# State-space scan with a feed-forward layer on one core: new durations in the table from which the order of issue is planned

## Chip, cores and metric

One core of one Trainium2 chip. The metric is the device time of one execution in microseconds (us), smaller is better. The kernel before takes 324.34 us (median of 3 runs, 323.94 to 324.47).

## What is computed

A linear state-space scan in chunks, and a feed-forward layer on its output. From the reference:

```python
batch, n_heads, seq, head_dim, d_state = (4, 8, 768, 32, 16)   # x, a, B, C in float32
for c in range(nc):                    # chunks along the sequence
    cum = np.cumsum(log(a)[c], axis=-1)
    L = np.exp(cum[:, :, :, None] - cum[:, :, None, :]) * causal
    y = (np.einsum('bhin,bhjn->bhij', Cc, Bc) * L) @ xc  +  (Cc @ state) * np.exp(cum)
    state = exp(sum(la)) * state + sum_j exp(cum[-1] - cum[j]) * B[j] x[j]
# x: (3072, 256) from y;  w_in (256, 2048), w_out (2048, 256): float64 in, float32 arithmetic here
h = x @ w_in
g = h - np.tanh(h)
out = g @ w_out
```

## The kernel before

**The scan.** The sequence is cut into 28 chunks (4 batches, 7 chunks of at most 112 tokens). The state of the chunk before enters a chunk as 16 extra rows of its `x` tile. TensorE makes, for chunks 0 to 3, the exponents of the decays (`cp`, lines 448 and 451) and the products of B and C (`att`, line 461). For chunks 4 to 9 one `att` tile gets both (lines 507 and 512). ScalarE takes the exponential into a tile `lt` (467, 516, 550), VectorE multiplies `lt` by `att` in place (471, 520, 684), GpSimd zeroes what is not causal (532, called the cut here), and TensorE multiplies `lt` by `x` into `y` (637, from chunk 10 on two chunks at once in 704) and the states into the next chunk's rows (644, or 572 into a tile `z`). `att` and `y` use the array in pieces of 32 rows or columns. ScalarE copies the new states into the rows of a later `x` tile (578 out of `z`, 650 out of `y`).

**The layer.** The output of the scan is split into a high and a low float32r half, `xh` by ScalarE (605, 617) and `xl` by VectorE (608, 619). 3,072 tokens are cut into 4 tiles of 256 and 4 of 512. For each tile and each of 16 slices of the hidden width, TensorE makes `ph` (763 with three products of halves, 756 in plain float32 for the first tile and the first weights), ScalarE takes tanh (794) and VectorE subtracts it (798) into `g`; `g` is split (802, 808), and TensorE adds `g` times w_out into `o` (844; 834 in plain float32 for the first weights). ScalarE copies partial sums out of `o` (872 into `pt`, 885).

**The weights.** They arrive as float64 words in `raw`, and are made into float32 by a chain: ScalarE 325, VectorE 330, 335, 338, 345. Then ScalarE makes the high half `wh` (349) and VectorE the low half `wl` (352). The first two of eight weight blocks are loaded and converted in two halves each, w_in first; the second half of these stays in float32 as `wf`.

**The order.** Nothing is issued as it is written. Each piece of work is first recorded with its engine, a duration in us, what it reads and what it writes:

```python
op("PE", 0.65, fn_p, r=[d["n_bc"], "lt_c", "rt_c"], w=[n_a])
op("ACT", 0.92, fn_e, r=[n_a], w=n_l)
op("DVE", 1.08, fn_m, r=[n_a], w=n_l)
op("POOL", 1.4, lambda: cut(ck), w=n_l)
```

`Order.schedule` (line 136 on) plays these records against each other: an engine takes, of the work that is ready, the piece with the smallest priority; a transfer occupies one common lane for bytes / `RATE` after a fixed start, and its data may be used `DMA_LATENCY` later. `Order.search` repeats this forward and backward 16 times with priorities jittered by a random generator (`SEED`), and keeps the pass that ends first; `issue` then emits every instruction in the order of its start. On the chip each engine, and SyncE's queue of transfers, works through its own instructions strictly in this order. A planned start is not enforced: only the order is, and semaphores hold an instruction until its inputs, and the buffer that it writes, are free. Buffers that matter below: two banks `ph`, one bank each of `po0`, `po1` (for `z`, `y` and `o` in turn) and one set of banks `att`, so that the next `att` waits until VectorE has read the last one.

Of the kernel before, what the change touches and what calls it, by code (L numbers as in the profile page):

```python
# [63 lines left out]
class Order:  # L64
# [3 lines left out]
    DMA_LATENCY, SEM, SEM_PE, RATE, FLIGHT = 0.8, 0.15, 0.28, 0.32e6, 8  # L68
    ROUNDS, JITTER, SEED, EARLY, LOOK = 16, 0.3, 266, 8.0, 0.5
# [19 lines left out]
    def __call__(self, eng, cost, fn, r=(), w=(), dma=0, after=(), urge=0.0):  # L89
# [33 lines left out]
        if dma:  # L123
            self.urge.append(urge)

            self.ops.append(("DMA", max(0.25, dma / self.RATE), None, {i: 1.4, **{j: 0.0 for j in chain}}))
# [9 lines left out]
    def schedule(self, prio, back=False, hold=None):  # L136
# [18 lines left out]
        while done < n:  # L155
# [67 lines left out]
def tile_ssm_moe(ctx: ExitStack, tc: tile.TileContext, a, x, bn, bc, wts, out):  # L223
# [90 lines left out]
    def conv(u, halves=False):  # L314
# [63 lines left out]
    def prep(G):  # L378
# [18 lines left out]
        op("POOL", 0.3, fn_c, r=["idn"], w=[d["n_bc"]])  # L397
        if near:
            op("POOL", 0.8, fn_b, r=["wdec", "bi", d["n_b"]], w=[d["n_bw"]])
# [35 lines left out]
    def first_tile():  # L435
# [38 lines left out]
        for ck in range(FIRST):  # L474
# [5 lines left out]
            for i in range(2):  # L480
                n_f, n_k = slot("ph", NPH), slot("g", 3)
                op("POOL", 0.7, lambda ck=ck, i=i: fn_k(ck, i), r=["la"], w=[n_k], urge=urge)
                op("PE", 1.14, lambda ck=ck, i=i: fn_f(ck, i), r=[n_k, "upto", "never"], w=[n_f])
                op("ACT", 0.52, lambda ck=ck, i=i: fn_x(ck, i), r=[n_f, "tab"], w=[k["n_l"][i]], urge=urge)
# [9 lines left out]
    def chunk_a(ck):  # L494
# [27 lines left out]
        op("PE", 0.65, fn_p, r=[d["n_bc"], "lt_c", "rt_c"], w=[n_a])  # L522
# [12 lines left out]
    def chunk_l(ck):  # L535
# [87 lines left out]
    def chunk_y(ck):  # L623
# [29 lines left out]
        cost = 0.48 if apart else 0.68  # L653
# [35 lines left out]
    def pair_y(ck):  # L689
# [51 lines left out]
    def mm1(t, f):  # L741
# [32 lines left out]
        op("PE", 12 * rate(w) * blocks(t), fn, r=[*n, f"wh{f // 2}.0", f"wl{f // 2}.0"], w=[n_h])  # L774
# [43 lines left out]
    def mm2(t, f, seg):  # L818
# [30 lines left out]
        if native(t, f):  # L849
            op("PE", 6.8 * 0.25 * blocks(t) / 2, fn, r=[*n_in, f"wf{f // 2}"], w=n_po[t, seg])  # L850
# [164 lines left out]
    for w in range(2):  # L1015
        op("DVE", 0.85, lambda w=w: signs(w), r=["par"], w=["rt_c"])
# [47 lines left out]
    op("PE", 0.95, sums_rows, r=["la", "upto"], w=[n_pr])  # L1064
    op("PE", 0.55, lambda: sums_cols(upto, "pq"), r=["la", "upto"], w=[n_pr])
# [3 lines left out]
    op("DVE", 1.4, lambda: [split(i) for i in range(1, 6) if i != 4], r=["rows"], w=["parts"])  # L1069
# [6 lines left out]
    op("ACT", 0.22, lambda: nc.scalar.activation(wdec.rearrange("p h c -> p (h c)"), misc["pq2"][:, 0:NHC], AF.Exp),  # L1076
# [123 lines left out]
```

## Time and profile before

| | |
|---|---|
| median of 3 runs | 324.34 us |
| the profiled execution, its own time | 324.25 us |
| its span | 322.6 us |
| TensorE, matmuls | 313.7 us, 97% of the span |
| VectorE | 215.3 us, 67% |
| ScalarE | 210.3 us, 65% |
| GpSimd | 60.6 us, 19% |
| transfers | 35.27 MB |

The span counts from the first to the last instruction of the core; 1.65 us of the time lie around it. Engines are named PE (TensorE), DVE (VectorE), ACT (ScalarE), POOL (GpSimd) and SP (SyncE, which issues transfers). L763 is line 763 of the kernel. A matmul on 4-byte data shows as two instructions in the trace where the order has one. Busy times of TensorE overlap from one matmul to the next; the chain of waits counts end to end instead.

### The profile page before, as it was taken

How to read it: one execution, taken by the hardware profiler on the slowest of the kernel's cores; microseconds unless marked ns; L12 is line 12 of the kernel's file. 1: busy time of each engine (PE TensorE's matmuls, PEld its weight loads, DVE VectorE, ACT ScalarE, POOL GpSimd, SP SyncE). 2: the span in 40 equal slices, each digit the busy share in tenths (PEclk: the TensorE clock that was granted, in tenths of full speed). 3: DMA queues.
4: the chain of work that ended last, by engine and by line, in shares of the span. 5: the costliest groups of instructions: out<-in, count | busy, mean ns of one | idle time of the engine just before them, and what ended most of it. 6: DMA issues, size and time to landing. Idle time of an engine off the chain costs nothing.

```text
span 322.6 us, 5757 instructions
## 1 busy us (share of the span) xinstructions
PE 313.7 (97%) x2160; PEld 255.3 (79%) x2160; DVE 215.3 (67%) x314; ACT 210.3 (65%) x471; POOL 60.6 (19%) x94
## 2 busy tenths in 40 slices
PE   8997999999999999999999999999999999999995
PEld 7765888788888878787878887888878788888883
DVE  6978997898888867457563864664765645645552
ACT  6568888477687888575945854966868544534451
POOL 8604424003122514402300400111102000000000
PEclk9999999999999999999999999999999999999999
DMA  6679557539433149280606005005420000100001
GB/s 205 195 238 325 173 162 307 183 94 346 89 65 66 30 98 272 48 241 5 205 0 207 16 0 209 1 2 226 168 61 0 2 0 0 68 1 0 2 0 65
DMA packets 15451, 35.27 MB, mean 109 GB/s; under 512 B 2464, under 2 KB 4416, under 8 KB 15424
## 3 DMA queue, kind: packets, MB, share of 16 engines
q1 hardware_dynamic: 13696, 31.76, 29.4%
q0 software_dynamic: 1728, 3.15, 5.7%
q8 instruction: 17, 0.28, 0.4%
q14 instruction: 10, 0.08, 0.1%
HBM read 28.32 MB, written 3.43 MB: 98 GB/s over the span
## 4 chain that ended last, share of the span: by engine, by line
PE 91%; DVE 5%; ACT 2%; issue 1%
PE ph L763 39%; PE o L844 38%; PE o L834 3%; PE y L704 3%; PE att L678 3%; PE y L637 1%; PE warm L1003 1%; DVE lt L471 1%; ACT lt L550 1%; DVE lt L520 1%; DVE wv L345 1%; PE att L461 1%; PE cp L451 1%; ACT lt L516 1%; DVE wm L338 1%
## 5 line engine op out<-in xcount | busy, mean ns | idle before, releaser
L798 DVE TENSOR_TENSOR g<-ph,g 128x512 f32<-128x512 f32 x96 | 65.7, 688 | 52.1 <-ACT g L794 52.0
L794 ACT ACTIVATE g<-ph 128x512 f32<-128x512 f32 x96 | 57.3, 598 | 48.7 <-PE ph L763 47.8
L808 DVE TENSOR_TENSOR gl<-g,gh 128x512 fp32r<-128x512 f32 x88 | 62.7, 715 | 31.0 <-ACT gh L802 29.5
L763 PE MATMUL ph<-xh,wh 128*128 128x512 f32 (+1 forms) x200 | 76.0, 382 | 0.0
L763 PE MATMUL ph<-xh,wl 128*128 128x512 f32 (+1 forms) x200 | 74.8, 377 | 0.0
L802 ACT CAST gh<-g 128x512 fp32r<-128x512 f32 x88 | 54.4, 620 | 28.3 <-DVE g L798 26.4
L844 PE MATMUL o<-gh,wh 128*128 128x512 f32 x176 | 69.2, 393 | 0.0
L844 PE MATMUL o<-gl,wh 128*128 128x512 f32 x176 | 68.5, 389 | 0.0
L844 PE MATMUL o<-gh,wl 128*128 128x512 f32 x176 | 68.5, 389 | 0.0
L763 PE MATMUL ph<-xl,wh 128*128 128x512 f32 (+1 forms) x200 | 59.0, 376 | 0.0
L532 POOL TENSOR_SCALAR_AFFINE_SELECT lt<-lt 128x896 f32<-128x896 f32 (+1 forms) x24 | 23.3, 969 | 128.4 <-ACT lt L550 118.3
L763 PEld LDWEIGHTS ph<-xh,wh 128*128 128x128 f32 x200 | 37.6, 188 | 7.6 <-issue 0.6
L763 PEld LDWEIGHTS ph<-xh,wl 128*128 128x128 f32 x200 | 37.6, 188 | 6.8
L763 PEld LDWEIGHTS ph<-xl,wh 128*128 128x128 f32 x200 | 36.7, 188 | 7.0
L550 ACT ACTIVATE lt<-lt,ncum 128x112 f32<-128x112 f32 (+1 forms) x144 | 41.7, 375 | 0.0
L844 PEld LDWEIGHTS o<-gh,wh 128*128 128x128 f32 x176 | 33.0, 188 | 7.8 <-issue 0.8
L844 PEld LDWEIGHTS o<-gl,wh 128*128 128x128 f32 x176 | 33.0, 188 | 6.9
L844 PEld LDWEIGHTS o<-gh,wl 128*128 128x128 f32 x176 | 33.1, 188 | 6.7
L684 DVE TENSOR_TENSOR lt<-att,lt 128x896 f32<-128x896 f32 (+1 forms) x18 | 18.9, 1052 | 0.0
L888 POOL DMA_DIRECT2D pt<-part x12 | 11.1, 1023 | 41.1 <-ACT part L885 38.1
L834 PE MATMUL o<-g,wf 128*128 128x256 f32 x64 | 15.4, 384 | 1.4 <-ACT x L578 0.9
L605 ACT CAST xh<-y 128x224 fp32r<-128x224 f32 (+4 forms) x18 | 7.3, 413 | 13.1 <-DVE s L711 10.6
(97 smaller groups left out, 275.0 us busy)
## 6 DMA issues: line engine op xcount, KB each, us to landing
lt<-cumr SPq DMA_DIRECT2D x18, 512.0 KB
raw<-w_d SPq DMA_DIRECT2D x16, 512.0 KB
bc<-bc_d SPq DMA_DIRECT2D x14, 352.0 KB
x<-x_d SPq DMA_DIRECT2D x14, 256.0 KB
pt<-part POOLq DMA_DIRECT2D x12, 256.0 KB, 4.5
out_d<-ob SPq DMA_DIRECT2D x8, 256.0 KB
braw<-bn_d SPq DMA_DIRECT2D x14, 112.0 KB
out_d<-pt SPq DMA_DIRECT2D x4, 256.0 KB
```

Of the source, the lines that this page charges most:

```text
L532: nc.gpsimd.affine_select(out=k["l"][:, :, 0:q], in_=k["l"][:, :, 0:q], pattern=[[0, H], [1, q]], compare_op=ALU.is_ge, fill=0.0, base=N, ...
L550: nc.scalar.activation(k["l"][:, h, 0:q], k["l"][:, h, 0:q], AF.Exp, bias=ncum[:, h, ck : ck + 1])
L678: nc.tensor.matmul(out=a_[:, i], lhsT=bb[r], rhs=cc[r, :, 0 : qlen(ck)], start=True, stop=True)
L684: nc.vector.tensor_tensor(out=l, in0=chs[j]["a"], in1=l, op=ALU.mult)
L763: nc.tensor.matmul(out=ph[:, i * w : i * w + w], lhsT=w_[:, u, 0, k, j * P : (j + 1) * P], rhs=(xh, xl)[p][:, k, ts], start=p == 0 and k = ...
L794: nc.scalar.activation(g[:, 0:used], gs[t, f][0][:, 0:used], AF.Tanh)
L798: nc.vector.tensor_tensor(out=g, in0=ph, in1=g, op=ALU.subtract)
L802: nc.scalar.copy(gh[:, 0:used], gs[t, f][1][:, 0:used])
L808: nc.vector.tensor_tensor(out=gl[:, 0:used], in0=g[:, 0:used], in1=gh[:, 0:used].bitcast(F32), op=ALU.subtract)
L834: nc.tensor.matmul(out=po[t, seg][e], lhsT=wf[:, u, 256 * j + e * P : 256 * j + (e + 1) * P], rhs=gs[t, f][1][:, i * w : i * w + w], start ...
L844: nc.tensor.matmul(out=po[t, seg][e], lhsT=w_[:, u, 1, j, e * P : (e + 1) * P], rhs=g[:, i * w : i * w + w], start=f == seg[0] and k == 0 ...
L888: op("POOL", 1.0, lambda e=e: nc.gpsimd.dma_start(out=pts[m][:, e], in_=obs[t, e], accum_op=ALU.add), r=[name, n_pt[2 * m], n_pt[2 * m + 1 ...
```

## The change

No instruction is added or removed. The recorded durations are replaced, the fixed start of a transfer becomes a name of its own (1.4 us before, now 0.65 us, with 0.45 us instead of 0.8 us behind the data and a lower rate), and the seed of the search is another. With other numbers the search ends in another order. The core of the diff (some 25 more durations change like the last ones shown):

```diff
-    DMA_LATENCY, SEM, SEM_PE, RATE, FLIGHT = 0.8, 0.15, 0.28, 0.32e6, 8
-    ROUNDS, JITTER, SEED, EARLY, LOOK = 16, 0.3, 266, 8.0, 0.5
+    DMA_START, DMA_LATENCY, SEM, SEM_PE, RATE, FLIGHT = 0.65, 0.45, 0.15, 0.28, 0.29e6, 8
+    ROUNDS, JITTER, SEED, EARLY, LOOK = 16, 0.3, 2, 8.0, 0.5
...
-                start[i + 1] = max(free["DMA"], end + 1.4)
+                start[i + 1] = max(free["DMA"], end + self.DMA_START)
...
-        op("POOL", 1.4, lambda: cut(ck), w=n_l)
+        op("POOL", 0.97, lambda: cut(ck), w=n_l)
...
-            op("PE", 6.88 * 0.25 * blocks(t) / 2, fn, r=[*n, convs[f // 2]], w=[n_h])
+            op("PE", 7.7 * 0.25 * blocks(t) / 2, fn, r=[*n, convs[f // 2]], w=[n_h])
```

What the new numbers do is seen in the order of each engine. In the rows below a line has the line number, the operation, what is written <- what is read, and the shape; a number at the end of a name is that of the buffer, and counts up in each program by itself.

**First place: SyncE's queue at the very start**, right after the load of `a`: the loads of B and C (`bc`), of `x`, of the first half of the first weights (`raw`, 512 KB) and of B again (`braw`). Before:

```order
L265 DMA bc_136<-bc_d 128x704
L265 DMA bc_138<-bc_d 128x704
L296 DMA raw_147<-w_d 128x1024
L277 DMA x_156<-x_d 128x512
L277 DMA x_158<-x_d 128x512
L265 DMA bc_160<-bc_d 128x704
L286 DMA braw_106<-bn_d 112x256
```

Now:

```order
L265 DMA bc_136<-bc_d 128x704
L277 DMA x_151<-x_d 128x512
L265 DMA bc_154<-bc_d 128x704
L296 DMA raw_159<-w_d 128x1024
L286 DMA braw_106<-bn_d 112x256
L277 DMA x_165<-x_d 128x512
L265 DMA bc_171<-bc_d 128x704
```

One `x` load (256 KB) now stands ahead of the first weights, and `braw` has come forward.

**Second place: VectorE and ScalarE while chunks 4 to 6 and the second weight block are worked on** (some 23 to 32 us of the trace before). `lt_433` before is `lt_430` now, chunk 5; `lt_513` is `lt_516`, chunk 6; `g_0_408` is `g_0_482`, the first slice of the layer; `wm` and `wv` belong to the conversion of the second weight block. VectorE before:

```order
L345 SCALAR_TENSOR_TENSOR wv_389<-wv_389,wm_410 128x512
L520 TENSOR_TENSOR lt_433<-att_416,lt_433 128x8x112
L798 TENSOR_TENSOR g_0_408<-ph_0_377,g_0_408 128x512
L330 TENSOR_SCALAR wm_410<-raw_328 128x512
L335 TENSOR_SCALAR wv_389<-wv_389 128x512
L338 SCALAR_TENSOR_TENSOR wm_410<-wv_389,wm_410 128x512
L619 TENSOR_TENSOR xl<-xf,xh 128x2x336
L520 TENSOR_TENSOR lt_513<-att_491,lt_513 128x8x112
L608 TENSOR_TENSOR xl<-y_453,xh 128x2x112
L345 SCALAR_TENSOR_TENSOR wf<-wv_389,wm_410 128x512
```

VectorE now:

```order
L345 SCALAR_TENSOR_TENSOR wv_388<-wv_388,wm_407 128x512
L520 TENSOR_TENSOR lt_430<-att_413,lt_430 128x8x112
L330 TENSOR_SCALAR wm_407<-raw_338 128x512
L335 TENSOR_SCALAR wv_388<-wv_388 128x512
L338 SCALAR_TENSOR_TENSOR wm_407<-wv_388,wm_407 128x512
L798 TENSOR_TENSOR g_0_482<-ph_0_375,g_0_482 128x512
L619 TENSOR_TENSOR xl<-xf,xh 128x2x336
L345 SCALAR_TENSOR_TENSOR wf<-wv_388,wm_407 128x512
L608 TENSOR_TENSOR xl<-y_450,xh 128x2x112
L520 TENSOR_TENSOR lt_516<-att_490,lt_516 128x8x112
```

ScalarE before, where `x_412` and `x_473` are the `x` tiles into which states are copied:

```order
L516 ACTIVATE lt_383<-att_365 128x8x112
L325 ACTIVATE wv_389<-raw_328 128x512
L794 ACTIVATE g_0_408<-ph_0_377 128x512
L578 COPY x_314<-z_391 16x2x64 x4
L516 ACTIVATE lt_433<-att_416 128x8x112
...
L605 CAST xh<-y_453 128x2x112
L617 CAST xh<-xf 128x2x336
L578 COPY x_412<-z_435 16x2x64 x4
L794 ACTIVATE g_2_503<-ph_2_476 128x512
L516 ACTIVATE lt_513<-att_491 128x8x112
L650 COPY x_473<-y_453 16x64 x4
```

ScalarE now (`x_409` and `x_467` are those tiles):

```order
L516 ACTIVATE lt_383<-att_363 128x8x112
L617 CAST xh<-xf 128x2x336
L325 ACTIVATE wv_388<-raw_338 128x512
L578 COPY x_253<-z_390 16x2x64 x4
L516 ACTIVATE lt_430<-att_413 128x8x112
...
L605 CAST xh<-y_450 128x2x112
L794 ACTIVATE g_0_482<-ph_0_375 128x512
L578 COPY x_409<-z_432 16x2x64 x4
L794 ACTIVATE g_2_503<-ph_2_471 128x512
L650 COPY x_467<-y_450 16x64 x4
L516 ACTIVATE lt_516<-att_490 128x8x112
```

`g_0` has moved on VectorE from ahead of three conversions to behind them, and the exponential of chunk 6 on ScalarE from ahead of the copies out of `y` to behind them. The load of `x_409` is issued ahead of a 352 KB load of `bc` now; `x_412` was issued behind it.

**Third place: TensorE from the first `o` on** (29.90 us before). Before:

```order
L834 MATMUL o_0_0_505<-g_0_408,wf 128x256 x4
L507 MATMUL att_524<-rt_c,lt_c 128x224
...
L512 MATMUL att_524<-bc_340 128x224 x4
L637 MATMUL y_537<-lt_433,x_314 32x112 x8
L644 MATMUL y_537<-x_314,bw_375 16x32 x8
L763 MATMUL ph_0_558<-xh,wh 128x256
...
L834 MATMUL o_0_0_505<-g_2_503,wf 128x256 x4
```

Now:

```order
L834 MATMUL o_0_0_507<-g_0_482,wf 128x256 x4
L637 MATMUL y_522<-lt_430,x_253 32x112 x8
L644 MATMUL y_522<-x_253,bw_380 16x32 x8
L763 MATMUL ph_0_539<-xh,wh 128x256
...
L507 MATMUL att_568<-rt_c,lt_c 128x224
...
L512 MATMUL att_568<-bc_350 128x224 x4
L834 MATMUL o_0_0_507<-g_2_503,wf 128x256 x4
```

`att` of chunks 7, 8 and 9 stood together with a `y`; now each stands alone between `ph` and `o`. From 60 us on TensorE's order is the same but for a few short stretches in which a `ph` stands one block earlier or later.

## Rows read from the trace of the kernel before

**Rows 1.** The page's table of engines (busy time, share of the span, instructions) and, from its 40 equal slices of the span (8.07 us each), the transfer rate.

```profile
PE 313.7 (97%) x2160; PEld 255.3 (79%) x2160; DVE 215.3 (67%) x314; ACT 210.3 (65%) x471; POOL 60.6 (19%) x94
...
GB/s 205 195 238 325 173 162 307 183 94 346 89 65 66 30 98 272 48 241 5 205 0 207 16 0 209 1 2 226 168 61 0 2 0 0 68 1 0 2 0 65
```

**Rows 2.** The chain of waits (start us, us, engine and line): its last piece.

```profile
318.77 0.69 DVE ob L908
```

**Rows 3.** The waits of TensorE, whole span (line that waited <- what ended the wait: us in total, times, longest us).

```profile
PE o L834 <- ACT x L578: 0.9, 1, 0.9
...
PE z L572 <- POOL bc L395: 0.8, 1, 0.8
PE att L507 <- DVE lt L520: 0.6, 1, 0.6
PE o L834 <- DVE g L798: 0.5, 1, 0.5
```

**Rows 4.** The chain of waits, 9 to 14 us (start us, us, engine and line).

```profile
9.14 0.47 DVE wm L330
9.61 0.34 DVE wv L335
...
11.02 0.69 DVE wv L345
11.71 1.11 DVE lt L471 x2
...
12.86 0.70 PE att L461 x8
```

**Rows 5.** Two instructions that waited for a transfer: ScalarE's timeline, then GpSimd's (start us, us, engine, line, operation, out<-in, in brackets the idle time before it and what ended it).

```profile
8.36 0.68 ACT L325 ACTIVATE wv<-raw 128x512 f32<-128x512 f32 x1 [0.90 <-DMA raw<-w_d]
...
10.86 0.21 POOL L395 COPY bc<-idn 128x32 f32<-128x32 f32 x1 [0.42 <-DMA bc<-bc_d]
```

**Rows 6.** VectorE's timeline, 23 to 33 us (columns as in rows 5).

```profile
23.26 0.42 DVE L330 TENSOR_SCALAR wm<-raw 128x512 uint32<-128x512 uint32 x1
...
24.78 1.51 DVE L345 SCALAR_TENSOR_TENSOR wv<-wv,wm 128x512 uint32<-128x512 uint32 x1
26.21 1.08 DVE L520 TENSOR_TENSOR lt<-att,lt 128x896 f32<-128x896 f32 x1
27.21 0.68 DVE L798 TENSOR_TENSOR g<-ph,g 128x512 f32<-128x512 f32 x1
27.81 0.82 DVE L330 TENSOR_SCALAR wm<-raw 128x512 uint32<-128x512 uint32 x1
...
29.00 0.69 DVE L338 SCALAR_TENSOR_TENSOR wm<-wv,wm 128x512 uint32<-128x512 uint32 x1
29.61 0.85 DVE L619 TENSOR_TENSOR xl<-xf,xh 128x672 fp32r<-128x672 f32 x1
31.31 1.09 DVE L520 TENSOR_TENSOR lt<-att,lt 128x896 f32<-128x896 f32 x1 [0.85 <-ACT lt L516]
32.32 0.38 DVE L608 TENSOR_TENSOR xl<-y,xh 128x224 fp32r<-128x224 f32 x1
```

**Rows 7.** GpSimd's timeline, the two cuts that run beside those conversions.

```profile
24.77 0.98 POOL L532 TENSOR_SCALAR_AFFINE_SELECT lt<-lt 128x896 f32<-128x896 f32 x1
...
27.37 0.99 POOL L532 TENSOR_SCALAR_AFFINE_SELECT lt<-lt 128x896 f32<-128x896 f32 x1
```

**Rows 8.** ScalarE's timeline: 28 to 32 us, and 55 to 56 us.

```profile
28.78 1.07 ACT L578 COPY x<-z 16x128 f32<-16x128 f32 x4 [1.19 <-DMA x<-x_d]
29.87 0.60 ACT L794 ACTIVATE g<-ph 128x512 f32<-128x512 f32 x1
30.37 0.91 ACT L516 ACTIVATE lt<-att 128x896 f32<-128x896 f32 x1
31.16 0.83 ACT L650 COPY x<-y 16x64 f32<-16x64 f32 x4
...
55.37 0.57 ACT L872 COPY pt<-o 128x512 f32<-128x512 f32 x1
55.84 0.59 ACT L794 ACTIVATE g<-ph 128x512 f32<-128x512 f32 x1
```

**Rows 9.** SyncE's timeline of transfers issued (start and us of the issue, not of the transfer).

```profile
19.29 0.53 SPq L265 DMA_DIRECT2D bc<-bc_d  x1
23.60 0.33 SPq L277 DMA_DIRECT2D x<-x_d  x1
```

**Rows 10.** TensorE's timeline (columns as in rows 5).

```profile
29.90 1.99 PE L834 MATMUL o<-g,wf 128*128 128x256 f32 x8 [0.86 <-ACT x L578]
...
51.61 0.30 PE L644 MATMUL y<-x,bw 128*16 128x32 f32 x16
51.84 1.99 PE L834 MATMUL o<-g,wf 128*128 128x256 f32 x8
...
57.21 1.99 PE L834 MATMUL o<-g,wf 128*128 128x256 f32 x8 [0.50 <-DVE g L798]
```

**Rows 11.** The chain of waits on TensorE: 46 to 51 us.

```profile
46.31 0.52 PE y L637 x16
...
46.95 1.63 PE ph L763 x12
48.57 1.73 PE o L834 x8
```

More of the change, by code (lines that the diff above doesn't have):

```diff
@@ L124, in __call__ @@
             self.urge.append(urge)
-            self.ops.append(("DMA", max(0.25, dma / self.RATE), None, {i: 1.4, **{j: 0.0 for j in chain}}))
+            self.ops.append(("DMA", max(0.25, dma / self.RATE), None, {i: self.DMA_START, **{j: 0.0 for j in chain}}))
             for n in r:
@@ L395, in fn_c @@
             nc.gpsimd.tensor_copy(out=bb[:, :, 0:N], in_=idn.unsqueeze(1).broadcast_to([P, CPG, N]))
-        op("POOL", 0.3, fn_c, r=["idn"], w=[d["n_bc"]])
+        op("POOL", 0.22, fn_c, r=["idn"], w=[d["n_bc"]])
         if near:
-            op("POOL", 0.8, fn_b, r=["wdec", "bi", d["n_b"]], w=[d["n_bw"]])
+            op("POOL", 0.64, fn_b, r=["wdec", "bi", d["n_b"]], w=[d["n_bw"]])
     def qlen(ck):
@@ L481, in first_tile @@
                 n_f, n_k = slot("ph", NPH), slot("g", 3)
-                op("POOL", 0.7, lambda ck=ck, i=i: fn_k(ck, i), r=["la"], w=[n_k], urge=urge)
-                op("PE", 1.14, lambda ck=ck, i=i: fn_f(ck, i), r=[n_k, "upto", "never"], w=[n_f])
-                op("ACT", 0.52, lambda ck=ck, i=i: fn_x(ck, i), r=[n_f, "tab"], w=[k["n_l"][i]], urge=urge)
+                op("POOL", 0.63, lambda ck=ck, i=i: fn_k(ck, i), r=["la"], w=[n_k], urge=urge)
+                op("PE", 1.1, lambda ck=ck, i=i: fn_f(ck, i), r=[n_k, "upto", "never"], w=[n_f])
+                op("ACT", 0.55, lambda ck=ck, i=i: fn_x(ck, i), r=[n_f, "tab"], w=[k["n_l"][i]], urge=urge)
                 if i == 0:
@@ L557, in chunk_l @@
         if ck < NCK - NB:
-            op("POOL", 0.6, fn_b, r=["wdec", "bi", d["n_b"]], w=n_l)
-        op("ACT", 2.2, fn_e, r=["ncum", "tab"], w=n_l)
-        op("POOL", 1.1, lambda: cut(ck), w=n_l)
+            op("POOL", 0.42, fn_b, r=["wdec", "bi", d["n_b"]], w=n_l)
+        op("ACT", 2.34, fn_e, r=["ncum", "tab"], w=n_l)
+        op("POOL", 0.97, lambda: cut(ck), w=n_l)
     def state(G):
@@ L578, in fn_c @@
             nc.scalar.copy(to, d["z"][D * i : D * i + N, 0 : 2 * D * CPG].rearrange("p (c e) -> p c e", c=CPG))
-        op("PE", 0.55, fn, r=[*d["p_x"], d["n_bw"]], w=[n_z])
+        op("PE", 0.36, fn, r=[*d["p_x"], d["n_bw"]], w=[n_z])
         for i in range(4):
-            op("ACT", 0.22, lambda i=i: fn_c(i), r=[n_z], w=grp[G + NB // CPG]["p_x"])
+            op("ACT", 0.26, lambda i=i: fn_c(i), r=[n_z], w=grp[G + NB // CPG]["p_x"])
     def parts_of(ck, n, yv, n_y, **kw):
@@ L652, in chunk_y @@
         r, w = [*k["n_l"], d["p_x"][cg], *([] if apart else [d["n_bw"]])], [n_y]
-        cost = 0.48 if apart else 0.68
+        cost = 0.45 if apart else 0.64
         if ck == JOINT - 1:
@@ L771, in mm1 @@
             n = sorted({"xf" + k[2:] for k in n})
-            op("PE", 6.88 * 0.25 * blocks(t) / 2, fn, r=[*n, convs[f // 2]], w=[n_h])
+            op("PE", 7.7 * 0.25 * blocks(t) / 2, fn, r=[*n, convs[f // 2]], w=[n_h])
             return
-        op("PE", 12 * rate(w) * blocks(t), fn, r=[*n, f"wh{f // 2}.0", f"wl{f // 2}.0"], w=[n_h])
+        op("PE", (12 if 2 * w > BANK else 12.7) * rate(w) * blocks(t), fn, r=[*n, f"wh{f // 2}.0", f"wl{f // 2}.0"], w=[n_h])
     def native(t, f):
@@ L849, in mm2 @@
         if native(t, f):
-            op("PE", 6.8 * 0.25 * blocks(t) / 2, fn, r=[*n_in, f"wf{f // 2}"], w=n_po[t, seg])
+            op("PE", 7.5 * 0.25 * blocks(t) / 2, fn, r=[*n_in, f"wf{f // 2}"], w=n_po[t, seg])
         else:
@@ L1006, in tile_ssm_moe @@
     op("ACT", 1.4, lambda: table(0), w=["tab"])
-    op("POOL", 1.6, consts_pool, w=["upto", "after", "pid"])
+    op("POOL", 1.1, consts_pool, w=["upto", "after", "pid"])
     op("POOL", 1.0, masks, w=["never"])
     op("DVE", 0.25, logs, r=["al"], w=["a"])
-    op("ACT", 0.4, lambda: nc.scalar.activation(la.rearrange("p h (c b) -> p c b h", b=NB), a_sb, AF.Ln), r=["a", "tab"], w=["la"])
-    op("DVE", 1.2, consts_dve, r=["pid"], w=["idn", "par"])
+    op("ACT", 0.6, lambda: nc.scalar.activation(la.rearrange("p h (c b) -> p c b h", b=NB), a_sb, AF.Ln), r=["a", "tab"], w=["la"])
+    op("DVE", 0.65, consts_dve, r=["pid"], w=["idn", "par"])
     op("ACT", 1.4, lambda: table(1), r=["la"], w=["tab"])
@@ L1015, in tile_ssm_moe @@
     for w in range(2):
-        op("DVE", 0.85, lambda w=w: signs(w), r=["par"], w=["rt_c"])
+        op("DVE", 0.75, lambda w=w: signs(w), r=["par"], w=["rt_c"])
     for G in range(2):
@@ L1063, in tile_ssm_moe @@
     n_pr = slot("po1", 1)
-    op("PE", 0.95, sums_rows, r=["la", "upto"], w=[n_pr])
-    op("PE", 0.55, lambda: sums_cols(upto, "pq"), r=["la", "upto"], w=[n_pr])
+    op("PE", 0.53, sums_rows, r=["la", "upto"], w=[n_pr])
+    op("PE", 0.38, lambda: sums_cols(upto, "pq"), r=["la", "upto"], w=[n_pr])
     op("DVE", 0.33, lambda: nc.vector.tensor_scalar(out=ncum.rearrange("p h c -> p (h c)"), in0=misc["pq"][:, 0:NHC],
@@ L1068, in tile_ssm_moe @@
     op("DVE", 0.36, lambda: split(0), r=[n_pr], w=["rows"])
-    op("DVE", 1.4, lambda: [split(i) for i in range(1, 6) if i != 4], r=["rows"], w=["parts"])
+    op("DVE", 2.2, lambda: [split(i) for i in range(1, 6) if i != 4], r=["rows"], w=["parts"])
     for i in range(2):
```

8 lines of the change are left out of this document (4 added, 4 removed).

## The prediction, made before the changed kernel ran

> **What bounds the kernel now.** I read the table of engines first. TensorE is busy for 313.7 of 322.6 us, and no other engine passes 67% [rows 1]. No matmul is added or removed, so the time can only change where TensorE waits, where a matmul costs more for its neighbour, and in the tail. The tail is one copy that follows the last matmul, at 318.77 us [rows 2], and a store; its order is the same. So I read TensorE's waits next. From 20 us on there are four of half a microsecond or more that matter here: 0.8 before `z`, 0.9 before the first `o`, 0.6 before an `att`, and 0.5 before a later `o` [rows 3]. The last stands at 57.21 us [rows 10]. Behind it TensorE runs for 261 us without a wait in that list. What an order can win or lose is therefore decided in the first 57 us, and the rest keeps its length unless a new wait arises there. The chain of waits then tells who holds TensorE early: up to 12.8 us it runs through VectorE's conversion of the first weight half, from 9.14 on, and through multiplications that hand over to `att` [rows 4].
>
> **The change, part by part.** The reordering is followed forward through the four engines with the durations of the trace; each part is given as its difference at TensorE.
>
> *First weights later.* The first `raw` half now has 256 KB more ahead of it in SyncE's queue. Before, ScalarE waited for it until 8.36 us, and GpSimd for the third `bc` until 10.86; between the two 864 KB landed, in 2.5 us, or 345 KB per us [rows 5]. At that rate 256 KB take 0.75 us; at the 205 GB/s of the first slice [rows 1] 1.28 us. I take 0.8, since the first rate is that of the same loads, hence a landing at 9.15. ScalarE's 0.68 us on it [rows 5] ends at 9.8. VectorE's line 335 needs that result and started at 9.61 [rows 4]. So VectorE's chain, and TensorE behind it, is 0.2 us late; bounds 0 and 0.7.
>
> *The first `o`.* It started at 29.90, after 0.86 us of waiting for ScalarE's line 578 [rows 10]. That instruction empties `z` out of the bank that `o` needs, and it had waited 1.19 us for the load of `x` into which it copies [rows 8]. This load was issued at 23.60, behind a `bc` load of 352 KB issued at 19.29 [rows 9]. Now it goes ahead of that `bc`: 352 KB at 345 KB per us is 1.0 us, so it lands near 27.7. ScalarE was ready for it at 27.59 (28.78 less the wait), with line 617 just ahead; a tanh takes the place of line 617 now, so it is ready at about the same time, starts at 27.7 and has emptied the bank by 28.8. This wait goes; what is late next is `g_0`. Its subtraction stood right behind chunk 5's multiplication, at 27.21 [rows 6], and now comes after lines 330, 335 and 338. On VectorE: chunk 4's multiplication and the conversion behind it are 0.2 late, so chunk 5's multiplication starts at 26.4 instead of 26.21, and ends its slot at 27.4. Lines 330 and 335 take 1.19 (27.81 to 29.00), line 338 takes 0.61 (29.00 to 29.61) [rows 6], so `g_0` starts at 29.2 and ends its 0.68 at 29.9. The first `o` starts at 29.95: **+0.05 us**. The waits before it change places rather than go. Bounds: VectorE on time, TensorE itself arrives at 29.04 (29.90 less the wait), so -0.86; with a late first weight half and one more conversion stretched by 0.8 (below), +1.3.
>
> *The wait before `att`.* The chunk 6 multiplication was late (31.31, after 0.85 idle) because its exponential stood behind the delayed line 578, at 30.37 [rows 6, 8]. In the new order TensorE wants that `att` only after `o`, `y` and `ph`: 29.95 + 1.95 + 0.64 + 1.63 [rows 10, 11], or 34.2. ScalarE: line 578 to 28.8, tanh of `g_2` 0.60, line 650 0.83, line 516 0.91 [rows 8], done at 31.1. Line 650 now stands ahead of that exponential, and waits for its own `x`: this load and the `bc` are 608 KB behind 27.7, or 29.5 at the same rate, just when ScalarE is there. VectorE after `g_0`: lines 619 and 345 at 0.85 and 0.69, line 608 at 0.38, then 1.09 for the multiplication [rows 4, 6], done at 32.9. Cover 1.3 us. Thinner is the cover of the `y` before it, which needs the bank that line 608 reads: VectorE is through at 31.8, TensorE there at 31.9. **-0.56 us**; bounds -0.56 and 0.
>
> *Three more changes of array shape.* `att` and `y` run in pieces of 32 rows or columns, `ph` and `o` on the full array. An `o` right behind `ph` adds 1.73 us to the chain [rows 11]; behind a `y`, which ended at 51.91 (51.61 + 0.30), it ended at 53.83 [rows 10], or 1.92. So the step from pieces to the full array costs 0.19. For chunks 7, 8 and 9 the old order has one such step a cycle (`att`, `y`, `ph`, `o`), the new one two (`y`, `ph`, `att`, `o`). **+0.57 us**; bounds 0 and 0.8 (three times 0.26, the whole 1.99 against 1.73). The Trainium skill, in TensorEngine Tiling (Array Packing), Key Properties, says that a change of tiling mode drains TensorE; it gives no price. By that rule no neighbour hides the step and the term stands; without it the sum would be 0.57 us lower. The trace so far agrees, with the 0.19 us above.
>
> *The wait at 57 us.* That `o` waited 0.50 us for a `g` [rows 10], whose tanh stood behind a copy of partial sums (55.37, then tanh at 55.84) [rows 8]. The new ScalarE order has the tanh first. The copy still must empty the bank of that `o`, and is done by 56.5. TensorE comes at 56.71 less what is won. **-0.50 us**; bounds -0.50 and 0.
>
> The sum: 0.05 - 0.56 + 0.57 - 0.50 = -0.44 us against the profiled execution's own 324.25, or 323.81. The median of the runs is 0.09 above that execution, so 323.9. A measurement of this kernel tells about 0.2% or 0.65 us from no change: this is inside.
>
> **The rivals.** *The conversions lose their stretch: faster.* Line 345 took 1.51 us at 24.78 and line 330 0.82 at 27.81, where the same shapes take 0.69 [rows 4] and 0.42 [rows 6]. Each ran beside a cut on GpSimd (24.77 and 27.37, 0.98 and 0.99 us) [rows 7]. In the new order the first cut comes earlier, right behind chunk 4's multiplication, while VectorE's second conversion step must wait for ScalarE anyway (line 617 now stands before its line 325). If this hides both stretches, 0.82 and 0.40, then `g_0` is no longer last and TensorE is bound by itself: -1.2 more, 322.7; with the first alone, 323.1. For it: the order does separate cut and conversion somewhat. Against it: a cut still follows each multiplication, and a conversion stands there too. The Trainium skill, SBUF — State Buffer, Who interferes with whom, says that whichever of VectorE and GpSimd begins first holds the shared ports for its whole instruction; by that the stretch would move with the cut, and only what falls into a wait, some 0.4, would be gained: 323.5.
>
> *VectorE becomes the bound: slower.* Between 23.5 and 33 us VectorE has no idle time left in my walk, and `g_0`, which was ready 2 us early, now stands behind three conversion steps. Every slip there passes to TensorE in full. It decides once the first `o` starts after 31.05 (29.95 + 0.44 + 0.65). Two things can add up: a first weight half that lands by the slow rate (+0.5), and line 338 stretched beside GpSimd as line 345 was (+0.82). Together +1.3: 325.2. For it: the old trace shows such stretches, and idle time of 0.85 that the new order has no more [rows 6]. Against it: both ends at once are needed.
>
> **How the numbers follow.** The forecast, gains and costs that cancel to within 0.65 us, has 0.46. The faster rival has 0.34, since one stretch that is covered is enough for it; the slower one, which needs two things late at once, 0.20. Own range of the forecast: 323.7 to 324.9. The range of 8 in 10 reaches into both rivals: 322.8 to 325.2. Faster by over 0.2% 0.34, within 0.46, slower 0.20.
>
> **What would show it.** In the new trace: ScalarE's line 325 on the first `raw` begins near 9.15; TensorE's first `o` begins at 29.5 to 30.5, released by VectorE's line 798 rather than by line 578; no wait at the `att` of chunk 7 and none at 57 us; three single `att` groups, each followed by an `o` of about 1.92 us in the chain. It is wrong if line 578 again waits for `x`, if the first `o` starts before 29.2 or after 31, or if a wait of TensorE over 0.3 us appears after 60 us.

## Result and the profile after

The changed kernel takes 325.67 us (median, 325.31 to 326.12), the kernel before 324.02 on the same chip: a ratio of 1.0056, interval 1.0044 to 1.0068, or some 1.7 us slower. The prediction said 323.9 (own range 323.7 to 324.9) and no change. The profiled execution took 326.12 us with a span of 324.4; the numbers below are from it.

The page first: TensorE's busy time, the granted clock and the transfer rate, in the same 40 slices as before.

```profile
PE 315.4 (97%) x2160; PEld 256.0 (79%) x2160; DVE 216.5 (67%) x314; ACT 211.3 (65%) x471; POOL 60.2 (19%) x94
...
PEclk9997999999999999999999999999999999999999
...
GB/s 215 200 221 249 160 198 343 102 228 326 61 65 66 0 93 284 28 269 11 222 0 178 30 0 163 46 2 179 220 38 0 2 0 0 81 1 0 0 2 65
```

TensorE is 1.7 us longer busy than in [rows 1] with as many instructions; the 7 in the clock row, for 24 to 32 us, is the reason. Its waits (columns as in [rows 3]):

```profile
PE att L461 <- DVE lt L471: 2.0, 2, 1.4
PE ph L756 <- DVE wv L345: 1.1, 1, 1.1
...
PE z L572 <- POOL lt L532: 0.7, 1, 0.7
PE y L637 <- ACT xf L601: 0.5, 1, 0.5
```

The waits before the first `o`, the `att` of chunk 7 and the `o` at 57 us are gone, as predicted. Two others took their place, and both wait for a weight conversion on VectorE: `att` L461 through the multiplication behind the first one, `ph` L756 for the second one. TensorE's timeline shows the places:

```profile
21.80 0.27 PE L507 MATMUL att<-rt_c,lt_c 9*128 9x224 bf16 x4
...
26.01 0.42 PE L572 MATMUL z<-x,bw 128*16 128x32 f32 x31 [0.65 <-POOL lt L532]
...
28.04 3.68 PE L756 MATMUL ph<-xf,wv 128*128 128x256 f32 x8 [1.06 <-DVE wv L345]
...
32.26 1.99 PE L834 MATMUL o<-g,wf 128*128 128x256 f32 x8
...
59.13 1.97 PE L834 MATMUL o<-g,wf 128*128 128x256 f32 x8
```

The first `o` starts at 32.26 instead of 29.90 [rows 10], 2.36 later. The `o` that stood at 57.21 [rows 10] now starts at 59.13 without a wait, 1.92 later. The span is 1.8 longer. So in this execution everything was lost before the first `o`, 0.44 was won back between the two, and behind 60 us next to nothing happens.

VectorE's timeline tells who is late. First weight block:

```profile
9.49 0.90 DVE L330 TENSOR_SCALAR wm<-raw 128x512 uint32<-128x512 uint32 x1 [0.82 <-DMA raw<-w_d]
10.31 0.41 DVE L335 TENSOR_SCALAR wv<-wv 128x512 f32<-128x512 f32 x1
10.76 1.00 DVE L338 SCALAR_TENSOR_TENSOR wm<-wv,wm 128x512 uint32<-128x512 uint32 x1
11.79 1.18 DVE L345 SCALAR_TENSOR_TENSOR wv<-wv,wm 128x512 uint32<-128x512 uint32 x1
...
24.50 0.42 DVE L330 TENSOR_SCALAR wm<-raw 128x512 uint32<-128x512 uint32 x1
24.83 1.21 DVE L335 TENSOR_SCALAR wv<-wv 128x512 f32<-128x512 f32 x1
26.08 1.19 DVE L338 SCALAR_TENSOR_TENSOR wm<-wv,wm 128x512 uint32<-128x512 uint32 x1
27.30 0.69 DVE L345 SCALAR_TENSOR_TENSOR wv<-wv,wm 128x512 uint32<-128x512 uint32 x1
...
29.24 1.21 DVE L335 TENSOR_SCALAR wv<-wv 128x512 f32<-128x512 f32 x1
...
31.09 0.68 DVE L798 TENSOR_TENSOR g<-ph,g 128x512 f32<-128x512 f32 x1
```

The first block's last step ends at 12.97 instead of 11.71 (11.02 + 0.69, [rows 4]). The second block (24.50 to 27.99) takes 3.49 us; before, from 23.26 to 26.29 [rows 6], it took 3.03. In the third, one step takes 1.21, and `g_0` comes out only at 31.8. GpSimd's timeline for the same time:

```profile
24.66 1.10 POOL L532 TENSOR_SCALAR_AFFINE_SELECT lt<-lt 128x896 f32<-128x896 f32 x1 [4.04 <-DVE lt L520]
25.71 0.40 POOL L395 COPY bc<-idn 128x32 f32<-128x32 f32 x1
26.07 0.64 POOL L388 TENSOR_TENSOR bw<-braw,wdec 128x256 f32<-128x256 f32 x1
29.06 1.10 POOL L532 TENSOR_SCALAR_AFFINE_SELECT lt<-lt 128x896 f32<-128x896 f32 x1 [2.35 <-DVE lt L520]
```

Each long step of VectorE behind 24 us (24.83, 26.08, 29.24) begins just when a cut or `bw` has begun.

The clock, from the view by windows (columns: window, length, TensorE busy and count, granted clock, DMA share, GB/s):

```profile
24.00:28.00 4.00, 2.33 (x110) 1.00 0.49 156
28.00:32.00 4.00, 3.96 (x20) 0.57 0.94 319
```

The `ph` behind the wait of 1.06 ran at the lower level of 1.2 GHz: 3.68 us, where the `o` of the same shape takes 1.99 [rows 10]. This is not what made the kernel slower. Of the six executions this one has the lowest mean clock (0.995), the others have 0.998 to 1.0 and take 325.31 to 326.06; the two at 1.0 take 325.49 and 325.54, still 1.5 us above the kernel before. And without it TensorE would have waited: 28.04 + 1.99 and the `att` make 30.6, `g_0` was there at 31.8. The drop moved the first `o` by 0.5 in this execution.

### The profile page after: what moved, and what is told of

The parts are those of the page before. It is cut to its first block, busy times and chain, and to the rows that moved or that the text cites. A ratio compares the mean times of both kernels' runs of the same rounds, so it can differ in the third digit from the quotient of the medians.

```text
span 324.4 us, 5752 instructions
## 1 busy us (share of the span) xinstructions
PE 315.4 (97%) x2160; PEld 256.0 (79%) x2160; DVE 216.5 (67%) x314; ACT 211.3 (65%) x471; POOL 60.2 (19%) x94
## 4 chain that ended last, share of the span: by engine, by line
PE 92%; DVE 3%; DMA 2%; issue 1%; SPq 0%; ACT 0%
PE ph L763 40%; PE o L844 37%; PE o L834 5%; PE y L704 3%; PE att L678 3%; DMA raw<-w_d 2%; PE y L637 1%; PE ph L756 1%; DVE lt L471 1%; DVE wm L338 1%; PE att L512 1%; PE att L461 1%; DVE wv L345 1%; PE cp L451 1%; DVE wv L335 0%
## 5 line engine op out<-in xcount | busy, mean ns | idle before, releaser
L834 PEld LDWEIGHTS o<-g,wf 128*128 128x128 f32 x64 | 11.6, 189 | 2.8 <-issue 0.8
```

The costliest lines, as they stand in the source:

```text
L834: nc.tensor.matmul(out=po[t, seg][e], lhsT=wf[:, u, 256 * j + e * P : 256 * j + (e + 1) * P], rhs=gs[t, f][1][:, i * w : i * w + w], start ...
```

## Experiments

In all but runs 8 and 9 named pieces of recorded work are moved in the finished plan, so that only the order of issue changes (run 10 also leaves out two cuts; runs 8 and 9 search anew with another seed). A pair (a, b) issues a just before b; with a third entry 1, just behind it.

```diff
-        best = self.search()
-        start = best[1]
+        start = self.search()[1]
+        for a, b, *s in MOVES: start[self.ids[a]] = start[self.ids[b]] + (s or [-1])[0] * 1e-6
```

The names: `x`, `bc`, `braw` with a group of two chunks are loads; `scale`, `shift` are lines 325 and 330 of a weight block and half; `tanh`, `g`, `o` lines 794, 798, 834 of a tile and slice; `pt` line 872; `att`, `exp`, `mul`, `cut` those of a chunk; `bw` GpSimd's line 388; `xh`, `xl` lines 617, 619, and `("xl", 4)` line 608 of chunk 4. "Before" and "changed" name the kernel that a list is applied to; ratios are to the kernel before on the same chip.

**1. First weights ahead of `x` (changed).**

```diff
+MOVES = [(("x", 0), ("braw", 0))]
```

> The changed kernel, with one load moved: the first x load goes behind the first half of the first weights again, as in the kernel before. Theory W (the late weight half moves the whole head by the 1.24 us seen at the first att of chunk 4, and all of it reaches the end): ScalarE's line 325 starts near 8.4 and the time falls by 1.2 us, 324.4. Theory V (what counts at the first o is VectorE, with g_0 behind three conversion steps; the head is only part of it): g_0 moves with the head, the first o starts near 30.6 instead of 32.26, and 324.1 to 324.4 comes out as well; the two differ in the next runs. Theory K (the half clock during the second plain ph, 28.0 to 31.7 us, is the loss): the clock drops only behind the wait of 1.06 us before that ph; with that wait unchanged the drop stays and only 0 to 0.5 us are won, 325.2.

325.02 us, ratio 1.0028 (1.0013 to 1.0042). Half of the loss goes by the ratios, 0.65 us by the medians. `att` of chunk 4 starts 0.2 later than before; what is left sits in the same two places:

```profile
27.03 1.99 PE L756 MATMUL ph<-xf,wv 128*128 128x256 f32 x8 [1.06 <-DVE wv L345]
...
30.91 1.97 PE L834 MATMUL o<-g,wf 128*128 128x256 f32 x8 [1.28 <-DVE g L798]
```

VectorE's second conversion is as long as in the changed kernel (23.49 to 26.98, or 3.49 us), with the same two steps stretched:

```profile
23.82 1.21 DVE L335 TENSOR_SCALAR wv<-wv 128x512 f32<-128x512 f32 x1
...
25.07 1.18 DVE L338 SCALAR_TENSOR_TENSOR wm<-wv,wm 128x512 uint32<-128x512 uint32 x1
```

With the first weights in time, the second conversion and `g_0` hold TensorE by themselves. Theory W alone is not enough. Theory K does not hold either: the wait of 1.06 is the same, but in the profiled execution the clock did not fall (the `ph` took 1.99).

**2. Only the early loads of the change (before).**

```diff
+MOVES = [(("x", 0), ("bc", 1)), (("braw", 0), ("x", 1))]
```

> The kernel before, with the early loads in the order of the changed one (x of the first two chunks ahead of the second bc and the first weights, braw ahead of the second x). Theory W: the same 1.24 us late at the first att of chunk 4, and slower by 1.0 to 1.3 us, 325.1. Rival (the delay alone is swallowed, since the first o of this order waited for ScalarE's line 578 until 29.87 in any case, and VectorE had 0.85 us idle behind it): slower by 0.3 to 0.5, 324.4. [...]

325.21, ratio 1.0044 (1.0026 to 1.0062). The same start made late costs 1.2 us in the old order too. VectorE's first step stands at 9.64 behind a wait of 0.99 for `raw`, and `att` of chunk 4 is 1.28 late. So the lateness is real at TensorE, not 0.2. It came there without a stretch of VectorE's lines 338 and 345 (0.69 each): ScalarE stood for the same half, and the exponential behind line 325 in its queue (line 467) kept TensorE waiting. ScalarE's timeline, then TensorE's:

```profile
9.64 0.67 ACT L325 ACTIVATE wv<-raw 128x512 f32<-128x512 f32 x1 [1.66 <-DMA raw<-w_d]
...
11.04 0.35 PE L448 MATMUL cp<-never,eye 128*128 128x448 bf16 x1 [1.12 <-ACT lt L467]
```

**3. `g_0` ahead of the third conversion (changed).**

```diff
+MOVES = [(("tanh", 0, 0), ("scale", 1, 1)), (("g", 0, 0), ("shift", 1, 1))]
```

> The changed kernel, with the tanh of g_0 moved on ScalarE ahead of the second line 325 of the second weight block, and the subtraction of g_0 on VectorE ahead of the three conversion steps, both as in the kernel before. Theory V: g_0 is ready at 29.6 instead of 31.8, the first o starts as soon as TensorE is there (30.6 at full clock), and the time falls by 1.2 us to 324.3. Theory W alone: no gain from it, 325.5. Theory K: with the clock halved during the ph before it, TensorE comes only at 32.2 and nothing is gained in those executions.

325.41, ratio 1.0047 (1.0025 to 1.0068): 0.26 below the changed kernel by the medians, with intervals that overlap. The profiled execution again had a clock of 0.57 from 28 to 32 us, and its first `o` started at 32.42, no earlier. The times of the twelve executions part by the clock: six at 1.0 took 324.82 to 325.25, the six at 0.989 to 0.998 took 325.57 to 328.62. At 1.0 the move is thus worth some 0.65 (the changed kernel's two took 325.49 and 325.54), half of what theory V wanted; where the clock falls during the `ph`, the profiled execution shows no gain, as theory K said for such executions.

**4. Both moves (changed).** The lists of runs 1 and 3 together.

> The changed kernel with both moves (first weights ahead of x, g_0 ahead of the conversions). If W and V are both needed and add: the first o starts near 29.4, the wait before the att of chunk 7 and the one at 57 us stay away, and the three extra changes of array shape cost their 0.57: 323.0 to 323.3, faster than the kernel before. If only one of the two counts: 324.2 to 324.4, as that one alone.

324.54, ratio 1.0013 (1.0000 to 1.0026). With the weights in time `g_0` is worth 0.5 (against run 1). The theory wanted 323.0 to 323.3, the rival 324.2 to 324.4; the time is above both. The wait of 1.06 before `ph` L756 is still there (27.69), and a new one of 0.65 before the `y` of chunk 5. It also had no drop of the clock behind this same 1.06 (window 28 to 32 us):

```profile
28.00:32.00 4.00, 4.00 (x28) 1.00 0.89 329
```

**5 and 6. The two gains and the array changes by themselves (before).**

```diff
 # run 6
+MOVES = [(("tanh", 3, 0), ("pt", 2)), (("x", 3), ("bc", 4))]
 # run 5: the two of run 6, and
+         (("att", 8), ("o", 1, 0)), (("exp", 8), ("tanh", 1, 2), 1), (("mul", 8), ("g", 1, 2), 1), (("cut", 8), ("g", 1, 2), 1),
+         (("att", 9), ("o", 1, 2)), (("exp", 9), ("tanh", 2, 0), 1), (("mul", 9), ("g", 2, 0), 1), (("cut", 9), ("g", 2, 0), 1)
```

> The order before, with only two moves that the changed order also contains: the tanh of the g that TensorE waited 0.50 us for at 57.21 goes ahead of the copy of partial sums, and the load of x for chunk 6 goes ahead of the load of 352 KB of bc. Theory G (the gains that the prediction counted are there, and only other parts of the change lost them): the wait at 57 us goes, -0.50; the 0.86 before the first o shrinks to what g_0 allows, -0.6 to -0.86, some of which the wait of 0.56 before the next att gives back; together 323.0 or 0.8 to 1.0 below the kernel before. Rival (the waits are refilled by the next late thing): within 0.3 of the kernel before.

> The order before, with the two moves of the next run (tanh at 57 us ahead of the copy of partial sums, load of x for chunk 6 ahead of the load of bc), and in addition the products att of chunks 8 and 9 moved from ahead of y to behind ph, as the changed order has them, with their exponential, multiplication and cut. Theory A (each step from pieces of the array to the full array costs 0.19 us, whoever its neighbours are): two steps more, so 0.38 us slower than the next run, each o behind an att 1.92 us in the chain and not 1.73. Rival (the cost depends on something that lies elsewhere in the changed kernel): no more than 0.1 us slower than the next run.

Run 6: 323.82, ratio 0.9986 (0.9973 to 1.0000), some 0.45 us by the ratio, between the two theories, and 0.25 by the medians, which is the rival's; the interval allows both. The `o` at 57 us no longer waits (57.02). The wait before the first `o` is gone too, but another stands ahead of it:

```profile
27.46 1.99 PE L756 MATMUL ph<-xf,wv 128*128 128x256 f32 x8 [0.76 <-DVE wv L345]
...
29.99 1.99 PE L834 MATMUL o<-g,wf 128*128 128x256 f32 x8
```

In this execution the cut began 0.16 us behind the start of the second conversion (24.25 and 24.09), where the profile before has 1.51 (24.77 [rows 7] and 23.26 [rows 6]). It met line 335 (1.21) and `bw` met line 338 (1.01), in place of line 345 alone, and `ph` was late. So VectorE's conversion is next in line in the order before as well, and the same order on GpSimd and VectorE can put the cut beside one step or another.

Run 5: 324.06, ratio 1.0004 (0.9993 to 1.0015), 0.24 above run 6 by the medians and 0.0018 by the ratios. The chain of waits of run 6 and then of run 5, the same five `o` in each:

```profile
35.59 1.73 PE o L834 x8
40.19 1.73 PE o L834 x8
44.78 1.73 PE o L834 x8
48.77 1.73 PE o L834 x8
52.11 1.92 PE o L834 x8
```

```profile
35.94 1.73 PE o L834 x8
40.53 1.92 PE o L834 x8
45.32 1.92 PE o L834 x8
49.52 1.73 PE o L834 x8
52.85 1.92 PE o L834 x8
```

The two `o` that got an `att` ahead of them cost 1.92 instead of 1.73, the other three are unchanged, and the distance between the two chains grows from 0.35 to 0.74. In the chain theory A holds: 0.19 for each change of shape. The total (0.24 or, by the ratios, 0.6) agrees with its 0.38 only within the noise.

**7. Line 325 ahead of line 617 (changed, with the list of run 4).**

```diff
+MOVES = [..., (("scale", 1, 0), "xh")]
```

> The changed order with the two repairs of the fourth run (first weights ahead of x, g_0 ahead of the third conversion), and in addition ScalarE's line 325 of the second weight block back ahead of line 617. Theory S (VectorE's conversion is late because its steps run beside GpSimd's cut, and line 617 pushed them there): the second conversion takes 3.0 us again instead of 3.5, the second ph of the layer waits 0.5 or less instead of 1.06 us, and the time is 0.4 to 0.6 below the fourth run's 324.54, so 324.0. Rival (another step is stretched in its place, and the lateness stays): 324.4 to 324.6.

324.32, ratio 1.0011 (1.0000 to 1.0022). The conversion took 3.48 us: lines 335 and 338 still 1.21 and 1.18, and `ph` waited 1.06. ScalarE's order was not what put the steps beside the cut; the cut follows the multiplication on GpSimd as the conversion does on VectorE. The lateness stays, as the rival said.

**8 and 9. Table and seed exchanged.** Run 8 is the kernel before with `SEED` 2, run 9 the changed one with `SEED` 266.

> The table of durations before, unchanged, with the seed of the changed kernel (2). Theory T (the new durations make the order worse): within 0.6 us of the kernel before, 323.5 to 324.6. Rival (what decides is the draw of the search, not the table): 0.8 us or more away from it, up or down.

> The new table of durations with the old seed (266). Theory T (the table decides): within 0.6 us of the changed kernel's 325.67, 325.1 to 326.3. Rival (the draw of the search decides, since the old table with the new seed took 327.11): 0.8 us or more away from 325.67.

| | seed 266 | seed 2 |
|---|---|---|
| old table | 324.07 (before) | 327.11, 1.0114 (1.0075 to 1.0153) |
| new table | 325.57, 1.0061 (1.0047 to 1.0074) | 325.67, 1.0056 (1.0044 to 1.0068) |

Run 8 is the rival's, run 9 theory T's. For the new table both draws end at the same time, for the old one they lie 3 us apart. With seed 2 the new table is better than the old one, with 266 worse. But part of run 8's time is the clock: all six executions have a mean clock of 0.977 to 0.995, and in the profiled one (326.42, the lowest time) the clock fell behind a wait of TensorE of 1.9 us:

```profile
16.00:20.00 4.00, 4.00 (x27) 0.64 0.31 60
```

That is 0.36 of 4 us, or up to 1.4 us (an estimate from this row), so how far the old table with seed 2 lies from the new one at full clock is not shown. The kernel before was a good draw; that measured durations give worse orders does not follow. Run 9's order is another one and still waits 0.9 before its first `o` for line 578 and 1.1 for a `g` at 59 us. Two draws of each table are too few for more.

**10. No GpSimd beside the conversions (changed).** The cuts of chunks 4 and 5 are left out, `bw` is moved behind the cut of chunk 6.

```diff
+MOVES = [(("bw", 3), ("cut", 6), 1)]
-        op("POOL", 0.97, lambda: cut(ck), w=n_l)
+        op.ids["cut", ck] = op("POOL", 0.97, lambda: ck in (4, 5) or cut(ck), w=n_l)
```

> The changed kernel without the cuts of chunks 4 and 5 (their lt keeps its values above the diagonal), and with the product bw that GpSimd makes beside VectorE's second conversion moved behind the cut of chunk 6. Theory S (the conversion of the second weights, 3.50 us, is stretched by GpSimd beside it): its four steps take 2.1 to 2.2 us, the second ph of the layer starts 1.2 to 1.4 us earlier against the att ahead of it, g_0 another 0.8, so the time falls by 1.5 to 2.1 us, to 323.6 to 324.2. Rival (VectorE is slow there for a reason of its own, the load of transfers for one): the steps keep 3.3 us or more, and the time falls by no more than 0.5.

324.04, ratio 1.0010 (0.9998 to 1.0023): 1.5 us of the loss are gone by the ratios. VectorE's second conversion:

```profile
24.59 0.42 DVE L330 TENSOR_SCALAR wm<-raw 128x512 uint32<-128x512 uint32 x1
24.93 0.42 DVE L335 TENSOR_SCALAR wv<-wv 128x512 f32<-128x512 f32 x1
25.38 0.69 DVE L338 SCALAR_TENSOR_TENSOR wm<-wv,wm 128x512 uint32<-128x512 uint32 x1
26.11 0.69 DVE L345 SCALAR_TENSOR_TENSOR wv<-wv,wm 128x512 uint32<-128x512 uint32 x1
```

2.21 us instead of 3.49, while transfers were as dense (0.49 of the DMA engines in both). `ph` starts at 27.00 without a wait, the first `o` at 30.21 behind 0.61 for `g_0`. Theory S is shown. The 1.5 us is what all of GpSimd's stretch costs there, also the part that the kernel before has (3.03 instead of 2.21).

**11. `bw` later (before, with the list of run 6).** The list of run 6 and `(("bw", 3), ("cut", 6), 1)`.

> The sixth run's kernel (the order before with the tanh at 57 us and the x load moved), with the product bw moved on GpSimd from beside the second conversion to behind the cut of chunk 6. Theory S: the conversion meets the cut alone, 2.9 us and not 3.3, the wait of 0.76 before the second ph of the layer falls to 0.4, and 0.3 us of it reaches the end: 323.5. Rival (a later wait takes it up, the one before the att of chunk 7): 323.7 to 323.9, as the sixth run.

323.89, ratio 1.0005 (0.9990 to 1.0021), in the rival's range. In its profiled execution the load of `bc` for chunk 6 landed late, GpSimd began the cut only at 25.06, and line 345 was stretched (1.35): the conversion took 2.90, as the theory had it, but the `y` of chunk 5 then waited 1.15 for line 608.

**12. `bw` later (changed, with the list of run 4).**

> The changed order with first weights ahead of x, g_0 ahead of the third conversion (both as in the fourth run, 324.54), and the product bw moved behind the cut of chunk 6. Theory S: line 338 beside it takes 0.69 us again and not 1.18, the second ph starts 0.5 earlier, the time is 324.0 to 324.1. Rival: no more than 0.2 below the fourth run.

323.75, ratio 1.0006 (0.9996 to 1.0016). Line 338 takes 0.69 again and `ph` waits 0.57, as theory S had it. Against run 4 the time is 0.8 lower by the medians, which come from two chips, but 0.2 by the ratios, so what this is worth at the end stays unclear. Three moves (first weights, `g_0`, `bw`) take the changed order back to the kernel before, to within the interval.

**13 and 14. Two more steps off VectorE's queue.** Run 13 is run 12 and the first of these moves, run 14 all three.

```diff
+         (("xl", 4), "xl"),
+         (("shift", 1, 0), ("mul", 4)), (("scale", 1, 0), "xh")
```

> The twelfth run's kernel (323.75, a ratio to before of 1.0006), with VectorE's line 608 of chunk 4 moved ahead of lines 619 and 345. The y of chunk 5 waited 0.65 us there for line 608, which reads the bank that this y needs. Theory C (the lateness of the changed order is nothing but VectorE's queue between 24 and 33 us, so each step taken off it comes back at the end): the wait goes and the time falls by 0.5 to 0.65 us, 323.1 to 323.3, a ratio of 0.998 to 0.999. Rival (line 619, now later, holds the ph behind that y, or another part of the change holds the end): within 0.2 of the twelfth run, a ratio of 1.000 to 1.001.

> The run before this one, with line 330 of the second weights moved ahead of the multiplication of chunk 4, into the 0.79 us in which VectorE waits there for the exponential, and ScalarE's line 325 ahead of line 617. Theory C: the conversion behind the multiplication is 0.34 us shorter, the wait of 0.57 before the second ph falls by as much, and the time is 0.3 below the run before, 322.8 to 323.0. Rival (the cut on GpSimd then meets another step and stretches it by as much): no more than 0.1 below the run before.

Run 13: 323.56, ratio 0.9985 (0.9971 to 0.9999), theory C's by the ratio. The wait of 0.65 is gone; its profiled execution, 324.70 and above its median, waited 1.10 for a `g` at 57 us, behind a `raw` load on which VectorE stood for 1.52. Run 14: 323.06, ratio 0.9974 (0.9962 to 0.9987), the fastest of all, 0.8 us below the kernel before; against run 13 0.5 by the medians and 0.4 by the ratios, where theory C wanted 0.3 and the rival at most 0.1. TensorE's timeline there:

```profile
26.28 1.99 PE L756 MATMUL ph<-xf,wv 128*128 128x256 f32 x8
...
28.81 1.99 PE L834 MATMUL o<-g,wf 128*128 128x256 f32 x8
...
56.01 1.97 PE L834 MATMUL o<-g,wf 128*128 128x256 f32 x8
```

No wait before `ph`, none before `o`, 1.2 us ahead of [rows 10] at the last one. The stretch is still there (line 338, 1.35), but line 335 starts 1.01 us behind the multiplication's start, where run 12 has 1.34, and the conversion has room for it.

## Why the prediction was wrong

The term of the sum that failed is the +0.05 at the first `o`, and it was wrong by two sizes: the lateness of the first weights at TensorE (0.2), and the durations of VectorE's conversion steps. By the prediction's own sign (the first `o` after 31) the forecast fell.

*First weights later: a step that failed, by its size.* Predicted 0.2 at TensorE, bounds 0 and 0.7; measured 1.24 at the `att` of chunk 4 (21.80 against 20.56 before). Two things were missed. The half landed at 9.46 (the chain of waits has its transfer at 3.14 for 6.32 us), not at 9.15: the slow rate of the first slice held, which the text had as its other bound (1.28, measured 1.1). And the text went from the landing straight to line 335. Line 330 started 0.44 later (9.49 against 9.05), and then lines 330 and 345 took 0.90 and 1.18 where they had taken 0.56 and 0.69, beside GpSimd's work for the first chunks. That is 0.83, twice the lateness itself. Run 2 shows that TensorE is as late without this stretch, by way of ScalarE's queue, which the text did not follow. Runs 1 and 2 put 0.65 and 1.2 us of the end on these loads. The trace before was also the best case: in the ten profiled executions (of the two orders and their variants in runs 1 to 14, but for 8 and 9) that have no `x` load ahead of the first weights, the `att` of chunk 4 starts between 20.56 (before) and 21.45 (run 4), in the four that have one (changed, runs 2, 3 and 10) between 21.80 and 21.98. Median against median it is 0.95 late, still above the bound of 0.7.

*The first `o`.* Predicted +0.05, with -0.86 and +1.3; measured +2.36, 1.9 of it without the drop of the clock. The order of events was right: line 578 did not wait for `x` (it began at 28.02), and `g_0` behind three conversion steps came last. Two sizes were wrong: the 1.24 inherited from the first weights, and the stretch. `g_0` began at 31.09 and not at 29.2, 1.89 later: 1.04 of it is the first weights (1.24 less the 0.2), 0.46 the second conversion (3.49 for 3.03), 0.38 the way from chunk 5's multiplication to `g_0` (27.91 to 31.09, for 26.4 to 29.2). The text wrote the old durations of lines 330 to 345 into the new order, and kept more stretch for a bound. But who runs beside GpSimd changes with the order and with the moment. Before, GpSimd had line 395 of a later group ahead of the cut, waited there until 24.24 and began the cut at 24.77 [rows 7], so one step of the second conversion was hit. Now the cut stands first and comes 0.16 us behind the conversion's start, with `bw` close behind it; two steps are hit, and one of the third conversion. Here too the trace before was kind: its order took 3.03, 3.48 and 3.31 us in three profiled executions (before, runs 5 and 6) and 3.38 in run 2, the changed one 3.48 to 3.49 in all five with `bw` in its place (changed, runs 1, 3, 4 and 7). So it is not the order alone that makes the stretch. Run 10 takes GpSimd away and finds 2.21 us. The Trainium skill, SBUF — State Buffer, Who interferes with whom, has it that whichever of the two engines begins first holds the shared ports for its whole instruction (for VectorE's steps in a two-port mode or with two inputs in SBUF). The trace agrees to 0.14 us: the cut of 24.66 ended at 25.76, and 0.42 more is 26.18; line 335 ended at 26.04.

*The wait before `att` of chunk 7, three array changes, the wait at 57 us:* -0.56, +0.57, -0.50, together -0.49. Measured between the first `o` and the one at 57: -0.44, and in run 1, where the clock did not fall, -0.46 (30.91 to 57.76). All three were right for this order, and run 5 shows the array term by itself. The cover that the text called thin is so: with `g_0` moved forward (runs 4, 7 and 12) the `y` of chunk 5 waits 0.65 for line 608. The chain of waits of the changed kernel has the three:

```profile
37.11 1.92 PE o L834 x8
...
41.90 1.92 PE o L834 x8
...
46.70 1.92 PE o L834 x8
```

*The rivals.* What happened is the slower one, VectorE as the bound, which was to decide once the first `o` starts after 31.05; it started at 32.26. Its price, 325.2, was 0.5 too low; it counted the late weights at 0.5 more, where 1.04 more was measured. It got 0.20 since the text asked for two things late at once. Both came, and neither was rare: the conversion was stretched in every profiled execution of the changed order that kept GpSimd's work there, also in run 1 with the weights in time. The faster rival (a stretch covered) was the opposite of what the order did.

*What stays open.* The moves of runs 1, 3 and 12 make up for the loss together; what each is worth alone is not one sum (0.65 for the first weights, 0.5 for `g_0` behind it, and for `g_0` alone 0.26 by the medians but 0.65 at full clock). Why the clock fell behind a wait of 1.06 in two profiled executions and not in runs 1, 4 and 7 behind the same wait was not found out.

## What to carry to other kernels

When an order changes, walk the engine that is nearest to being late with the durations that its steps have alone, and then set beside each the work of the engine that stretches it; a duration taken from a trace is that of its old neighbours, and of one execution. A lateness at the start is not an offset to be subtracted: follow it through every step to the engine that bounds the kernel. When a wait goes, look at what it hid (run 6), and before blaming a table of costs, run the search with another seed (runs 8 and 9).

## What the runs showed of the hardware

Steps of VectorE on 128x512 words of 32 bits took 0.42 (lines 330, 335) and 0.69 us (338, 345) with GpSimd idle, and up to 1.21 and 1.51 beside a GpSimd instruction of 0.64 to 1.44. Loads came at 215 KB per us in the first 8 us, and with a load of 256 KB ahead of it the next one landed 1.1 us later (9.46, against 8.36 before; run 11, without that load ahead, has 9.21), where later ones moved at 345. TensorE's granted clock was at 0.57 of full speed over 28 to 32 us in two profiled executions (changed and run 3), behind waits of 0.65 and 1.06 us, and at 1.00 in others with the same two waits (runs 1, 4 and 7).
